# One group of batch 1's first product in Strassen's form, batch 2's second half dealt to later slots, one slot skipped in batch 7's features

## The chip, the cores and the metric

The kernel runs on one core of a Trainium2 chip. Times are device microseconds (us) of a whole execution. Three runs of the kernel before gave 289.28, 289.88 and 290.69 us, a median of 289.88. One further execution was profiled. It took 289.9 us, of which the profile's span, from the first to the last instruction, is 288.1 us. Of the core's engines PE multiplies matrices, DVE (vector) and ACT (scalar) do elementwise work, POOL does casts and additions on data that is not in PSUM, and SP issues most of the DMAs.

## The reference

For each of 8 batches (8 heads, 576 positions, 64 channels a head) an attention without softmax is computed, and its output goes through a mixer with a low-rank step and two large products:

```python
q_p, k_p = phi(q, cos_w, sin_w), phi(k, cos_w, sin_w)    # relu(x)*cos and relu(x)*sin, side by side
kv  = einsum('bhsf,bhsd->bhfd', k_p, v);  z = sum(k_p, axis=2)
x   = einsum('bhsf,bhfd->bhsd', q_p, kv) / (einsum('bhsf,bhf->bhs', q_p, z)[..., None] + 1e-06)
u   = x + (x.T @ U @ V).T                                # x as (576, 512); rank 32
out = u + relu(u @ w_ch1) @ w_ch2                        # w_ch1: 512x2048, w_ch2: 2048x512
```

The first product, `u @ w_ch1`, and the second, with `w_ch2`, are most of the arithmetic.

## The kernel before, in words

**Tiling.** A batch's 576 positions are four chunks of 128 (c = 0 to 3) and a tail of 64 (c = 4). The 2048 hidden columns are 16 blocks j of 128. Chunks 0 to 3 of a batch run through the first product as 512 columns. The tails of two batches are put together as 128 columns and run by themselves (`g1_tail`, `g2_tail`).

**Slots.** The order of PE's work is written out by hand as a list of slots. `first_units(b)` lays the 16 slots of a batch's first product, `second_units(b)` the 14 half-parts of its second product, and `lay_all` puts them one behind the other. Batch 1's first product is slots 32 to 47, the tail product of batches 0 and 1 is 48 to 51, batch 1's second product is 52 to 65, the second tail product is 66 to 69, and batch 2's first product begins at slot 70. Everything else (features, attention, u, transposes, loads, forms) is put beside a slot by number: `put(at, ...)`. Each engine runs its instructions strictly in the order in which the slots and what lies beside them emit them; semaphores make it wait for the others.

**A first-product slot in plain form** is `g1_main(b, j)`: four matmuls of 512 columns into one PSUM bank of the pool `g` (three banks, `G3`), and a ReLU on ACT into `hid`. **A group m in Strassen's form** (`g1_part(b, m, part)`, seven parts) does four blocks j with 28 matmuls of 256 columns instead of 16 of 512. It needs four differences of u, `uT_form(b, n)` (line 608, tile `tb`), and four of the weights, `w1_form` (line 591, tile `sa`), both on DVE. The results of the parts 1, 6 and 5 are copied by ACT to `pw` (line 114), part 3 gets its ReLU on ACT, and the parts 2, 7 and 4 are finished by an addition on DVE (line 678) and, for odd batches, a ReLU on DVE (line 675). `MIXED` says which groups of which batch are in Strassen's form; the eight slots of such a half hold four plain blocks (`s4` to `s7`) and the seven parts.

**Batch b+1 beside batch b.** While batch 1 is in its products, the attention of batch 2 is done beside it. Its features (`q_prep`, `k_prep`, lines 305 and 307: ACT or DVE, one chunk and one of cos and sin at a time) come first, then `kv_pair` at slot 43 (40 matmuls, line 364, copied out by DVE, line 116), then five `x_unit`s (8 matmuls, line 439, and three DVE instructions, lines 429, 430, 449), then `A_unit` (line 465, copied out by ACT), `u_va` (line 495), two `u_add`s on DVE (line 506) and two DMA transposes of u to `uT` (line 535, on SP's queue). The transposes of q of the next batch (lines 408 and 413) go on the same queue. The second product (`w_part`, line 892) needs the forms of `hid` that DVE makes (`hid_form`, line 857).

Of the kernel before, what the change touches and what calls it, by code (L numbers as in the profile page):

```python
# [17 lines left out]
def kernel(  # L18
# [100 lines left out]
    V_, A_, G_ = nc.vector, nc.scalar, nc.gpsimd  # L119
# [478 lines left out]
    def uT_form(b, n):  # L598
        if b not in tb:
            tb[b] = pool.tile([P, 4, 2, 256], BF16, tag="tb", bufs=1, name="tb")  # L600
        t = tb[b]
        a, b_ = (
            (uT_block(b, 0, 1), uT_block(b, 0, 0)),
            (uT_block(b, 1, 1), t[:, 0]),
            (uT_block(b, 1, 1), uT_block(b, 0, 1)),
            (uT_block(b, 1, 0), t[:, 1]),
        )[n]
        V_.tensor_tensor(out=t[:, n], in0=a, in1=b_, op=ALU.subtract)
# [203 lines left out]
                in_=o_s[i * TS : i * TS + TS, :],  # L812
            )

    MIXED = {2: (0, 2), 3: (0, 2), 4: (0, 2), 5: (0, 2), 6: (0, 2)}
    FULL = [b for b, ms in MIXED.items() if 2 in ms and b > 2]
    HD = DM // 2
    KB = NJ // 2
# [209 lines left out]
    def loads(b):  # L1028
        def thunk(dst, src):
            def go():  # L1030
                load_tail(dst, src, b)
                load_main(dst, src, b)

            return go

        return thunk(qst, q), thunk(kst, k), thunk(vst, v)
# [5 lines left out]
    def lay(units, in_second):  # L1042
        slots.extend(units)
        second.extend([in_second] * len(units))
# [5 lines left out]
    def first_units(b):  # L1050
        starts[b] = len(slots)

        def unit(names, m):
            def go():
                for n in names:
                    if n[0] == "s":
                        g1_main(b, 4 * m + int(n[1]))
                    else:
                        g1_part(b, m, int(n))

            return go

        for m in (0, 2):
            if m in MIXED.get(b, ()):
                lay([unit(n.split(), m) for n in (HALF if b > 2 else HALF2)], False)
            else:
                lay([lambda j=j: g1_main(b, j) for j in range(4 * m, 4 * m + 8)], False)
        for i in range(4 * (0 < b)):
            n = 12 + 2 * i if b == 1 else (9, 11, 17, 18)[i] if b in MIXED and b > 2 else 8 + i + (b == 2)
            beside.setdefault(starts[b] + n, []).append(  # L1070
# [60 lines left out]
    def attention_plan(b):  # L1131
        plan = []
        odd = b % 2 == 1

        def put(at, f, *a):
            plan.append((at, lambda: f(b, *a)))

        ops = [(f, c, i) for f in (q_prep, k_prep) for c in QORD for i in range(2)]
        if b == 2:
            for n, (f, c, i) in enumerate(ops):  # L1140
                if n < 8:
                    put((25, 26, 27, 28, 28, 29, 29, 30)[n], feature, f, c, i, A_)
                elif n < 10:
                    put(24 + n, feature, f, c, i, V_)
                else:
                    put(
                        (34, 34, 35, 36, 37, 38, 39, 39, 40, 41)[n - 10], feature, f, c, i,
                        A_ if n in (14, 17) else V_,
                    )
            V0 = 33  # L1150
            at_q, at_load = (32, 34, 36), (37, 42, 43)
            kv_at, x_at, a_at, u_at = 43, (44, 46, 48, 50, 52), 54, 55
            a_bank = O1
        else:
            F, G = starts[b - 2] + (20 if odd and b < B - 1 else 16), starts[b - 1]
            late = b in (4, 6)
            both = (0, 1, 2, 8) if late else (0, 1, 2) if b == 7 else (0, 1, 2, 10, 11, 12) if b > 3 else (1, 2, 10, 11, 12)
            for s_ in range(G - F + 2 * late):
                for eng in (A_, V_)[: 1 + (s_ in both)]:
                    if ops:  # L1160
                        put(F + s_, feature, *ops.pop(0), eng)
            V0 = starts[b - 2] + 9 if b > 3 else F + 1
            at_q, at_load = (F + 7, F + 8, F + 8) if late else (F + 5, F + 7, F + 7), (F + 8, F + (16 if late else 14), V0 + (8 if late else 5))
            if b == 7:
                at_q = (F + 5, F + 11, F + 11)
            if b == 6:
                at_q, at_load = (F + 7, F + 12, F + 12), (F + 12, F + 16, V0 + 8)
            if b == 3:
                at_q = (F + 6, F + 7, F + 8)
                at_load = (F + 11, F + 14, F + 14)  # L1170
            X0 = G - 2 if odd else G
            x_at = [
                X0 + i for i in ((2, 4, 6, 9, 11) if b == 3 else (2, 4, 6, 8, 10) if odd else (3, 5, 7, 9, 11))
            ]
            kv_at = X0
            if late:
                kv_at, x_at = G + 3, [G + i for i in (5, 8, 13, 16, 18)]
            elif b - 1 in FULL:
                kv_at, x_at = G + 1, [G + i for i in ODDX]
            elif b > 3 and b - 1 in MIXED:  # L1180
                kv_at, x_at = G + 1, [G + i for i in X5]
            a_at = x_at[4] + (3 if b in (4, 6) else 3 if b == 3 else 2)
            u_at = a_at + 1
            a_bank = X1S if b == 3 else OB
        for n, c in enumerate(QORD):
            put(V0 + n, v_prep, 0, H, (c,), (G_,))
        for at_, (c0, c1) in zip(at_q, ((4, 5), (0, 2), (2, 4))):
            put(at_, qtr_dma, c0, c1)
        put(kv_at, kv_pair, *X1)
        for n, c in enumerate(ORD):  # L1190
            put(x_at[n], x_unit, c, *((O1, X1)[n % 2] if b < 4 else X1))
        put(a_at, A_unit, *a_bank, A_)
        put(u_at, u_va, (0, *X1), (2, *O1) if b < 4 else (2, OA, OB))
        d0 = 2 if odd and b - 1 in FULL else 0
        put(u_at, u_add, d0)
        put(u_at + 2, u_add, 2 - d0)
        put(u_at + 2, utr_dma, d0, d0 + 2)
        put(u_at + 4, utr_dma, 2 - d0, 4 - d0)
        if odd:
            late_t = 3 if b == 5 and b - 1 in FULL else 0 if b - 1 in FULL else 1 if b - 1 in MIXED else 0  # L1200
            put(u_at + 3 + d0 + late_t, u_tail, *X1S)
            put(u_at + 4 + d0 + late_t, utr_dma, 4, 5)
        if b < B - 1:
            for at_, t in zip(at_load, loads(b + 1)):
                plan.append((at_, t))
        return plan
# [233 lines left out]
    def put(at, thunk):  # L1440
        todo.setdefault(at, []).append(thunk)
# [3 lines left out]
    for n in range(4):  # L1445
        for m in (0, 2):
# [4 lines left out]
            )  # L1451
        for b in MIXED:
            put(starts[b] + (-3, -2, 0, 2)[n], lambda b=b, n=n: uT_form(b, n))
# [7 lines left out]
    for b in range(2, B):  # L1461
        for at, t in attention_plan(b):
            put(at, t)
# [35 lines left out]
```

## Time and profile before

| what | value |
|---|---|
| median of three runs | 289.88 us |
| profiled execution, its time | 289.9 us |
| profiled execution, its span | 288.1 us |
| PE busy | 281.1 us, 98% of the span |
| DVE busy | 221.9 us, 77% |
| ACT busy | 180.9 us, 63% |
| POOL busy | 71.3 us, 25% |
| PE's granted clock | 9 tenths or more in all 40 slices |

Times in the trace are counted from the start of the span. A row of the timeline has the start, the length, the engine, the line, the operation, what it writes and reads, and how many such instructions were merged. What stands in brackets is how long the engine had been idle before, and what ended that. PE is pipelined and the ends of its matmuls are modelled, so two rows of PE can overlap; the distance between the starts is what a group of matmuls really takes. The same holds in a smaller measure on DVE, where the next instruction starts some 0.08 us before the end that the row shows.

### The profile page before, as it was taken

What the parts mean: (1) busy time and instruction counts of PE and PEld (TensorE: products, weight loads), DVE (VectorE), ACT (ScalarE), POOL (GpSimd) and SP (SyncE); (2) the same over time, 40 slices, a digit from 0 to 9 for tenths busy, and PEclk for the clock granted to TensorE, in tenths of its full rate; (3) what the DMA queues carried; (4) which work ended last, traced back from release to release, by engine and by line L of the source; (5) the groups of instructions that cost most, each with busy time, mean ns of one, the idle gap of its engine ahead of it and who ended that gap; (6) DMA issues with size and microseconds to landing.
All of it is one profiled execution on the core that took longest, in us unless ns stands there. A gap on an engine that the chain in (4) does not pass through costs nothing. (4 is left out here: it accounts for less than half of the span.)

```text
span 288.1 us, 7603 instructions
## 1 busy us (share of the span) xinstructions
PE 281.1 (98%) x3108; PEld 212.1 (74%) x3134; DVE 221.9 (77%) x452; ACT 180.9 (63%) x319; POOL 71.3 (25%) x111
## 2 busy tenths in 40 slices
PE   8999999999999999999999999999999999999995
PEld 6776455545887767876987767876978778899884
DVE  4979739997888899658885498858884689689864
ACT  2975651576687588876686588876797772177110
POOL 8330600050008305640015500351015000400140
PEclk9999999999999999999999999999999999999999
DMA  6999999999999999899929991499959200610023
GB/s 201 337 284 252 289 208 251 284 178 154 281 213 190 239 362 184 212 269 250 257 54 198 321 304 43 89 152 183 299 69 233 99 0 11 156 75 2 2 86 132
DMA packets 85447, 53.32 MB, mean 185 GB/s; under 512 B 53990, under 2 KB 83078, under 8 KB 85414
## 3 DMA queue, kind: packets, MB, share of 16 engines
q1 hardware_dynamic: 78998, 41.62, 62.5%
q0 software_dynamic: 6272, 11.17, 16.3%
q8 instruction: 24, 0.39, 0.6%
q10 hardware_dynamic: 144, 0.07, 0.1%
q14 instruction: 9, 0.07, 0.1%
HBM read 36.86 MB, written 9.44 MB: 161 GB/s over the span
## 5 line engine op out<-in xcount | busy, mean ns | idle before, releaser
L710 PE MATMUL g_ps<-uT,w_bf 128*128 128x512 bf16 x264 | 67.5, 379 | 0.7
L717 ACT ACTIVATE hid<-g_ps 128x512 bf16<-128x512 f32 x72 | 42.6, 597 | 24.3 <-PE g_ps L710 21.5
L912 POOL TENSOR_TENSOR o_sb<-o_sb,u_bf 128x512 f32<-128x512 f32 x21 | 25.8, 1242 | 111.0 <-DVE o_sb L912 111.0
L892 PEld LDWEIGHTS <-hid 128*128 128x128 bf16 x448 | 43.0, 98 | 5.7 <-DVE hid L857 0.2
L678 DVE TENSOR_TENSOR hid<-pw,be_ps 128x512 bf16<-128x512 f32 x42 | 28.8, 686 | 17.8 <-PE be_ps L653 10.1
L710 PEld LDWEIGHTS <-w_bf 128*128 128x128 bf16 x282 | 26.2, 98 | 22.0
L892 PEld LDWEIGHTS <-S 128*128 128x128 bf16 x336 | 32.2, 98 | 4.4
L114 ACT ACTIVATE pw<-al_ps 128x512 f32<-128x512 f32 x42 | 24.9, 595 | 15.6 <-PE al_ps L653 9.8
L892 PE MATMUL w_ps<-T,hid 128*128 128x256 bf16 x224 | 27.9, 273 | 0.0
L892 PE MATMUL w_ps<-w_bf,hid 128*128 128x256 bf16 x224 | 27.8, 273 | 0.0
L892 PE MATMUL w_ps<-T,S 128*128 128x256 bf16 x224 | 27.1, 273 | 0.0
L114 ACT ACTIVATE o_sb<-w_ps 128x512 f32<-128x512 f32 x21 | 12.5, 597 | 20.4 <-PE w_ps L892 14.1
L912 DVE TENSOR_TENSOR o_sb<-o_sb,w_ps 128x512 f32<-128x512 f32 x21 | 14.4, 685 | 14.2 <-PE w_ps L892 7.5
L653 PEld LDWEIGHTS <-sa 128*128 128x128 bf16 x224 | 20.7, 98 | 5.3 <-issue 0.3
L506 DVE TENSOR_TENSOR u_bf<-x_bf,va_ps 128x1024 bf16<-128x1024 bf16 (+1 forms) x20 | 19.5, 1000 | 2.3 <-PE va_ps L495 2.3
L449 DVE TENSOR_TENSOR x_bf<-x_ps,rec 128x512 bf16<-128x512 f32 x28 | 19.4, 691 | 1.0
L653 PEld LDWEIGHTS <-w_bf 128*128 128x128 bf16 x168 | 16.3, 98 | 4.1 <-issue 0.2
L116 POOL CAST v_ext<-vst 128x512 bf16<-128x512 f32 x24 | 16.5, 727 | 7.3 <-issue 3.3
L305 ACT ACTIVATE k_p<-kst,sinw 128x512 bf16<-128x512 f32 x26 | 18.0, 712 | 0.4 <-DMA kst<-in_k_dram 0.4
L653 PE MATMUL al_ps<-tb,sa 128*128 128x256 bf16 x112 | 16.8, 273 | 0.3
L741 PE MATMUL gt_ps<-uT_tl,w_bf 128*128 128x128 bf16 x256 | 16.4, 219 | 0.0
L781 PE MATMUL o_ps<-w_bf,hid 128*128 128x512 bf16 x61 | 15.3, 379 | 0.2
(192 smaller groups left out, 513.5 us busy)
## 6 DMA issues: line engine op xcount, KB each, us to landing
qst<-in_q_dram SPq DMA_DIRECT2D x14, 512.0 KB, 6.1
kst<-in_k_dram SPq DMA_DIRECT2D x14, 512.0 KB, 8.1
vst<-in_v_dram SPq DMA_DIRECT2D x12, 512.0 KB, 9.7
out_dram<-o_sb POOLq DMA_DIRECT2D x12, 512.0 KB, 6.5
w_bf<-in_moe_w_ch_dram POOLq DMA_DIRECT2D x8, 512.0 KB, 11.0
out_dram<-o_sb SPq DMA_DIRECT2D x4, 512.0 KB, 3.0
qst<-in_q_dram SPq DMA_DIRECT2D x2, 640.0 KB, 5.7
kst<-in_k_dram SPq DMA_DIRECT2D x2, 640.0 KB, 13.8
```

What stands on the lines that cost most here:

```text
L114: nc.scalar.activation(out=o, in_=i, func=AF.Copy, bias=0.0, scale=1.0)
L116: eng.tensor_copy(out=o, in_=i)
L305: nc.scalar.activation(out=o, in_=i, func=AF.Relu, bias=0.0, scale=w)
L449: nc.vector.tensor_tensor(out=x_of(b, c, rows).rearrange("p (g i d) -> p g i d", g=2, d=D), in0=view[:, :, :, 0:D], in1=rec[rows].unsqueez ...
L506: nc.vector.tensor_tensor(out=u_bf[b][:, d0 : d0 + n], in0=x_bf[b].rearrange("p c (d n) -> p d c n", n=P)[:, d0 : d0 + n], in1=t.rearrange ...
L653: nc.tensor.matmul(out=res[:, k_, :], lhsT=lhs[:, d, k_, :], rhs=rhs[:, d, :], start=(opens and k_ == 0 and d == 0), stop=(k_ == 1 and d = ...
L678: V_.tensor_tensor(out=o, in0=x, in1=res, op=ALU.add)
L710: nc.tensor.matmul(out=g_ps.rearrange("p (c t) -> p c t", c=4), lhsT=w1_bf[:, d, j * P : j * P + P], rhs=uT[b][:, d, :, :], start=(d == 0) ...
L717: nc.scalar.activation(out=hid[b][:, j, :], in_=g_ps, func=AF.Relu, bias=0.0, scale=1.0)
L741: nc.tensor.matmul(out=g_ps[:, jj, :], lhsT=w1_bf[:, d, j * P : j * P + P], rhs=uT_tl[pr][:, d, :], start=(d == 0), stop=(d == 3),)
L892: nc.tensor.matmul(out=res[:, g, :], lhsT=lhs[:, k_, g * P : g * P + P], rhs=rhs[:, k_, :], start=(opens and k_ == 0 and g == 0), stop=(k_ ...
L912: eng.tensor_tensor(out=o_, in0=x, in1=y, op=ALU.add)
```

## The change

There are three parts.

1. `MIXED` gets the entry `1: (2,)`: the second group of eight blocks of batch 1 (slots 40 to 47) has its blocks 8 to 11 in Strassen's form. By the loop over `MIXED`, four `uT_form`s are put at the slots 29, 30, 32 and 34; the weight forms for this group were already there, for batch 2.
2. In batch 2's plan two feature steps of k are dealt to ACT at other places (steps 12 and 14 in place of 14 and 17), the fourth and fifth `x_unit` go from the slots 50 and 52 to 51 and 53, `A_unit` from 54 to 57 and `u_va` from 55 to 58. What hangs on `u_at` (the two `u_add`s and the two transposes) moves with it, to the slots 58 and 60 and 60 and 62. On SP's queue the first transpose of `u` now comes behind the next batch's transposes of q's tail and of the first half of q, and the second behind that of q's second half.
3. In batch 7's features the slot `F + 3` takes no feature, so that the features that followed come one slot later.

```diff
-    MIXED = {2: (0, 2), 3: (0, 2), 4: (0, 2), 5: (0, 2), 6: (0, 2)}
+    MIXED = {1: (2,), 2: (0, 2), 3: (0, 2), 4: (0, 2), 5: (0, 2), 6: (0, 2)}
...
                     put(
                         (34, 34, 35, 36, 37, 38, 39, 39, 40, 41)[n - 10], feature, f, c, i,
-                        A_ if n in (14, 17) else V_,
+                        A_ if n in (12, 14) else V_,
                     )
...
-            kv_at, x_at, a_at, u_at = 43, (44, 46, 48, 50, 52), 54, 55
+            kv_at, x_at, a_at, u_at = 43, (44, 46, 48, 51, 53), 57, 58
...
             for s_ in range(G - F + 2 * late):
+                if b == 7 and s_ == 3:
+                    continue
                 for eng in (A_, V_)[: 1 + (s_ in both)]:
```

## The prediction

> **What bounds the kernel now.** I read the busy shares first, then PE's waits, then the stretches around batch 1's first product.
>
> ```profile
> PE 281.1 (98%) x3108; PEld 212.1 (74%) x3134; DVE 221.9 (77%) x452; ACT 180.9 (63%) x319; POOL 71.3 (25%) x111
> ```
>
> ```profile
> PE w_ps L202 <- DVE zero L125: 1.2, 1, 1.2
> PE va_ps L495 <- ACT A_sb L114: 0.4, 1, 0.4
> PE xz L1219 <- ACT k_p L305: 0.4, 1, 0.4
> ```
>
> ```profile
> core 0: us, PE busy (x) PEld busy (x) DVE busy (x) ACT busy (x) POOL busy (x), PEclk, DMA share, GB/s
> 64.54:67.99 3.45, 3.45 (x17) 1.57 (x16) 2.95 (x7) 3.06 (x6) 0.00 (x0) 1.00 1.27 112
> 67.99:73.27 5.28, 5.23 (x72) 3.29 (x72) 3.43 (x9) 2.39 (x4) 0.00 (x0) 1.00 1.01 183
> 73.27:83.80 10.53, 10.53 (x173) 9.40 (x172) 9.26 (x19) 7.30 (x13) 0.00 (x0) 1.00 1.12 291
> ```
>
> PE is busy for 98% of the span, and the list of its waits has three entries, 2.0 us in all. So PE's own work sets the end: less of it is a gain one for one, and what any other engine does costs nothing until PE waits for it. Two of the waits are at the start; the middle one is a `u_va` that waits for ACT's copy of A, and part 3 of the change touches it. The stretches (batch 1's slots 40 to 43, 44 to 47, then the tail product and the first slots of the second product) show how near the others are to becoming the bound: DVE is busy for 2.95 of 3.45 us, 3.43 of 5.28 and 9.26 of 10.53. PE's clock is full throughout.
>
> **Part 1a, PE's work.** The chain that ended last has both kinds of matmul group without a wait between them:
>
> ```profile
> 223.93 0.44 PE al_ps L653 x4
> 226.54 0.86 PE g_ps L710 x4
> ```
>
> Four plain blocks are 4 x 0.86 = 3.44 us; the seven parts that replace them are 7 x 0.44 = 3.08. PE loses 0.4 us of work. All of it is gained ahead of `kv_pair`: the slots 40 to 43 held four blocks (3.44), and now hold the parts 1, 6, 2 and two blocks (3 x 0.44 + 2 x 0.86 = 3.04); the slots 44 to 47 go from 3.44 to 4 x 0.44 + 2 x 0.86 = 3.48.
>
> **Part 1b, DVE's new work ahead of `kv_pair`.** Four `uT_form`s come in at the slots 29 to 34. In the timeline (DVE, with the rows of the other engines that meet it):
>
> ```profile
> 55.88 0.60 ACT L114 ACTIVATE uT<-u 128x512 bf16<-128x512 f32 x1 [1.71 <-DVE uT L116]
> 56.36 0.42 DVE L591 TENSOR_TENSOR sa<-w_bf,sa 128x512 bf16<-128x512 bf16 x1
> 59.00 1.22 DVE L506 TENSOR_TENSOR u_bf<-x_bf,va_ps 128x1024 bf16<-128x1024 bf16 x1 [0.63 <-PE va_ps L495]
> 59.50 2.96 POOL L116 CAST v_ext<-vst 128x512 bf16<-128x512 f32 x4
> 60.14 1.10 DVE L833 TENSOR_TENSOR T<-w_bf 128x1024 bf16<-128x1024 bf16 x1
> 64.83 0.67 DVE L833 TENSOR_TENSOR T<-w_bf,T 128x1024 bf16<-128x1024 bf16 x1
> 67.02 0.47 DVE L307 TENSOR_SCALAR k_p<-kst,sinw 128x512 bf16<-128x512 f32 x1
> 69.42 0.70 DVE L116 CAST kv<-kv_ps 128x520 bf16<-128x520 f32 x1 [1.93 <-PE kv_ps L364]
> ```
>
> ```profile
> 63.68 4.48 PE L710 MATMUL g_ps<-uT,w_bf 128*128 128x512 bf16 x20
> 67.99 0.28 PE L364 MATMUL kv_ps<-v_ext,k_p 128*128 128x65 bf16 x4
> 69.20 1.03 PE L710 MATMUL g_ps<-uT,w_bf 128*128 128x512 bf16 x3
> ```
>
> What one form takes, and what an addition with its ReLU takes, is read from the starts in later batches, where they stand back to back, and the spread of the forms from their group:
>
> ```profile
> 94.36 0.41 DVE L591 TENSOR_TENSOR sa<-sa,w_bf 128x512 bf16<-128x512 bf16 x1
> 94.69 0.41 DVE L608 TENSOR_TENSOR tb<-uT,tb 128x512 bf16<-128x512 bf16 x1
> ...
> 134.31 0.68 DVE L678 TENSOR_TENSOR hid<-pw,be_ps 128x512 bf16<-128x512 f32 x1
> 135.03 0.29 DVE L675 TENSOR_SCALAR hid<-hid 128x512 bf16<-128x512 bf16 x1
> 135.24 0.69 DVE L857 TENSOR_TENSOR S<-S,hid 128x1024 bf16<-128x1024 bf16 x1
> ```
>
> ```profile
> L608 DVE TENSOR_TENSOR tb<-uT,tb x12: 411/420/1126, 94.7 to 253.5; 128x512 bf16<-128x512 bf16 x12
> ```
>
> A form takes 0.33 us from start to start, an addition with ReLU 0.93 (134.31 to 135.24). The first form also waits for ACT's copy of uT, which ends at 56.48, while DVE was free at 56.36: about 0.17 with the handover. So 4 x 0.33 + 0.17 = 1.5 us of new DVE time lies between 56.36 and the last `k_p` feature. The only slack there is the 0.63 us of idle time at 59.00; from there to 67.49 (67.02 + 0.47) DVE runs without a gap. The last feature, which `kv_pair` needs, ends 0.87 later, at 68.36. PE, which has gained 0.4, is at `kv_pair` at 64.54 + 3.04 = 67.58 (63.68 + 0.86 is the start of slot 40). It waits some 0.8 us and starts `kv_pair` at about 68.4 where it was 67.99: 0.4 later than before, the gain spent and as much again.
>
> Bounds: below, no wait at all, if DVE keeps pace (the slots 40 to 47 then end 0.4 earlier); above, forms as slow as some are beside POOL. `T` took 1.10 us while POOL cast v and 0.67 after; the slowest form took 1.126. One form, that of slot 34, falls where POOL's casts, themselves later behind a later store, will be; 0.3 to 0.4 more than 0.33 makes the start 68.8. I take 68.5, since three of the four lie ahead of the casts: +0.5 us. The Trainium skill (SBUF — State Buffer, Who interferes with whom) says that a DVE instruction with two SBUF inputs shares a read interface with a GpSimd instruction that reads SBUF, and that the one issued second is blocked until the first ends. Both inputs of a form are in SBUF, so by that rule the form of slot 34 waits for up to a whole cast, 0.74 (2.96 / 4), an estimate that would put the start at up to 69.1 and the sum at up to 290.6. The two rows of `T` agree with the rule's direction: 0.43 more beside the casts.
>
> The additions cost PE nothing here. The first (part 2) fits into the gap of 1.93 us ahead of the copy of kv. That copy ends 0.9 after PE has issued `kv_pair` (69.42 + 0.70 against 69.20), and PE has the parts 5 and 7 (0.88) in between. ACT's count in these slots stays the same, four copies or ReLUs for four ReLUs. Of the k features beside these slots ACT keeps two and DVE six; ACT's come two slots earlier, where the ReLUs of three banks of `g` cover them (if they didn't, PE would wait for one feature, 0.7), and DVE's end no earlier than reckoned above.
>
> **Part 2, the later half.** DVE gets two more additions with ReLU, 1.86 us, and is 0.5 late. It had 5.28 - 3.43 + 10.53 - 9.26 = 3.1 us of idle time up to 83.80. So it fits, but tightly. The nearest customers:
>
> ```profile
> 78.43 0.69 DVE L857 TENSOR_TENSOR S<-S,hid 128x1024 bf16<-128x1024 bf16 x1
> 82.05 1.05 PE L892 MATMUL w_ps<-T,S 128*128 128x256 bf16 x8
> ```
>
> S was ready at 79.12, 2.9 us before PE took it. DVE reaches it at most 0.5 + 1.86 later, at 81.5, and less by whatever of its idle time lies before. PE comes to it at 82.05 + 0.5 less A and `u_va`, which no longer stand before it (about 0.5 each, an estimate from the `u_va` row below, 0.40, and the change of operands): 81.5. So DVE is just in time, or early by the idle time, about 0.6 us. The `x_unit` ahead of A ends as much later; three slots (3 x 0.87) of delay for A cover that. I count part 2 as nothing on PE. What it does to SP's queue:
>
> ```profile
> 83.40 1.38 SPq L535 DMA_TRANSPOSE uT<-u_bf  x1
> 86.22 1.44 SPq L535 DMA_TRANSPOSE uT<-u_bf  x1
> 87.77 5.20 SPq L408 DMA_TRANSPOSE q_pT<-q_p  x2
> 93.03 1.00 SPq L93 DMA_DIRECT2D qst<-in_q_dram  x1
> 96.15 1.02 PE L710 MATMUL g_ps<-uT,w_bf 128*128 128x512 bf16 x4
> ```
>
> ```profile
> DMA to landing us min/median/max: 3.0/3.4/4.9
> DMA to landing us min/median/max: 4.3/5.1/11.8
> ```
>
> The first landing row is that of `uT`, the second that of `q_pT`. The first transpose of u moves from 83.40 by 2.6 + 0.5 to about 86.5 and holds SP to 87.9; the transpose of q's second half now follows (2.6, half of 5.20) to 90.5; the second transpose of u starts then, in place of 86.22, and lands at 93.5 to 95.4. The form that reads it would start at 94.69 + 0.5 = 95.2, PE's plain block at 96.15 + 0.5 = 96.6. With the median, 93.9, nobody waits; with the longest, DVE waits 0.2 and PE still nothing. The transposes of q are read only after slot 70, and the loads behind them on SP start about 1 us earlier than at 93.03; neither costs.
>
> **Part 3.**
>
> ```profile
> 209.89 0.71 ACT L305 ACTIVATE q_p<-qst,sinw 128x512 bf16<-128x512 f32 x1
> 210.98 0.27 ACT L114 ACTIVATE A_sb<-a_ps 128x128 bf16<-128x128 f32 x1
> 211.30 0.40 PE L495 MATMUL va_ps<-A_sb,V_bf 32*128 32x128 bf16 x16 [0.39 <-ACT A_sb L114]
> ```
>
> The feature at 209.89 now comes after A's copy. Taking 0.6 us away from ahead of that copy removes the 0.39 us that PE sat idle; what is late next is PE's own second product, so 0.39 is gained. ACT does the feature later, with more than a slot in hand before batch 7's kv. Bounds: 0 and 0.39.
>
> **Sum.** +0.5 (the net of -0.4 work and 0.9 wait) - 0.39 = +0.1 us against the profiled execution's 289.9, which stands with the median, 289.88. Forecast 290.0 us.
>
> **The rivals.** *DVE keeps pace, no wait at `kv_pair`*: -0.4 - 0.39 = -0.8, 289.1 us. For it: 0.5 us between the last feature and `kv_pair` in the trace, and forms at 0.33; against: DVE has no other gap after 59.00.
>
> *The second transpose of u lands late, slower.* It now waits behind a transpose of q, and those took up to 11.8 us to land. From a landing at 96.6 on PE waits for it, and DVE, which stands in order before the form, holds the additions behind it. With a landing as long as 7 us (90.5 + 7 = 97.5) PE loses 0.9 at its plain block and about as much again until DVE has caught up: 290.0 + 1.8 = 291.8. Against: no transpose of u took more than 4.9, and the next loads of q, k and v (from 93.03 before) stand behind it on SP.
>
> *Weight loads show.* There are 28 loads for 16, at 98 ns each (the 64.54 stretch has 1.57 us in 16); unhidden, twelve more cost 1.2 and the gain of 0.4 is no gain: 291.6. Against: 0.44 / 4 = 110 ns a matmul is no more than half of 0.86 / 4 = 215. The Trainium skill (TensorE: Matmul & The Clock Gate, Back-to-back issue gap) gives 131 ns for a sustained matmul of 512 columns and 81 for 128, by which 28 short ones would cost at least as much as 16 long ones (estimate 2.3 to 2.1 us); the trace's 215 and 110 do not agree.
>
> *Part 3 does nothing*, another copy holding ACT: 290.4.
>
> **How the numbers follow.** Forecast 0.55, DVE keeps pace 0.22, late transpose (or DVE's backlog reaching PE at S) 0.14, weight loads 0.02, part 3 without effect 0.07. The range goes from 288.8 (the gain of both, less the 0.3 that medians vary) to 291.6, and leaves out about 0.1 on either side together with the runs' scatter. 0.5%, 1.45 us, is about what can be told from no change. Faster than 288.4 needs more than the two gains together: 0.05. Slower than 291.3 is the late transpose, the weight loads, and a share of the forecast with several margins gone: 0.17. The rest, 0.78, is the same.
>
> **What the profile after would show.** A wait of PE at `kv_pair` (line 364) for a k feature on DVE, 0.7 to 1.2 us; 28 more matmuls of line 653 at 0.44 for four; no wait at line 495; no idle time of DVE between 59 and the copy of kv. Wrong would make it: no wait at line 364; a wait of line 710 or of DVE's forms for `uT` near 95; a wait of line 892 for S.

## The result, and the profile after

| | before | after |
|---|---|---|
| median of 22 runs each | 290.03 us | 290.60 us |
| lowest to highest | 289.28 to 291.88 us | 290.12 to 292.11 us |
| profiled execution: time, span | 289.9, 288.1 us | 290.39, 288.2 us |

The ratio of after to before is 1.0026, with a 95% interval of 1.0014 to 1.0038: the changed kernel is slower by 0.75 us (0.4 to 1.1; the two medians are 0.57 apart), less than the 0.5% that counts as a difference here. The forecast was 290.0. Three executions in the experiments below, two of part 3 alone (its profiled one among them) and one of the first two forms behind the additions, fell into a slower state of the chip (spans of 292.0 to 292.6 us) and are left out of all medians, ratios and readings.

The page of the changed kernel, its busy shares, and the list of PE's waits (engine, line, what it waited for, then us in total, times, longest):

```profile
span 288.2 us, 7669 instructions
...
PE 283.0 (98%) x3146; PEld 214.2 (74%) x3146; DVE 223.8 (78%) x462; ACT 180.8 (63%) x319; POOL 72.4 (25%) x111
```

```profile
PE w_ps L202 <- DVE zero L125: 1.2, 1, 1.2
PE kv_ps L364 <- DVE k_p L307: 0.3, 1, 0.3
PE g_ps L710 <- DVE o_sb L789: 0.2, 1, 0.2
```

PE's wait for ACT at line 495 is gone, and so is the one at line 1219, which lies at the start and comes and goes from run to run. Two new waits for DVE are there: the forecast one at `kv_pair`, and one at line 710, which no step of the prediction had. PE's busy time (281.1 before, 283.0 after) is no measure of its work here: the page before counts 3108 matmuls for 3134 weight loads, the page after 3146 for 3146, so some matmuls are missing from the first.

The single profiled executions differ in their starts and in late loads, so the spans alone tell little. A cleaner ruler is the stretch from the start of slot 32 (batch 1's first product) to the start of slot 70 (batch 2's). Before, from PE's timeline:

```profile
56.74 1.89 PE L710 MATMUL g_ps<-uT,w_bf 128*128 128x512 bf16 x8
...
95.45 0.60 PE L653 MATMUL al_ps<-uT,w_bf 128*128 128x256 bf16 x4
```

After:

```profile
56.86 1.03 PE L710 MATMUL g_ps<-uT,w_bf 128*128 128x512 bf16 x4
58.04 1.02 PE L710 MATMUL g_ps<-uT,w_bf 128*128 128x512 bf16 x4 [0.15 <-DVE o_sb L789]
...
64.97 0.60 PE L653 MATMUL al_ps<-uT,w_bf 128*128 128x256 bf16 x4
65.41 1.03 PE L710 MATMUL g_ps<-uT,w_bf 128*128 128x512 bf16 x4
...
68.04 0.26 PE L364 MATMUL kv_ps<-v_ext,k_p 128*128 128x65 bf16 x3
68.64 0.20 PE L364 MATMUL kv_ps<-v_ext,k_p 128*128 128x65 bf16 x1 [0.34 <-DVE k_p L307]
...
69.76 0.60 PE L653 MATMUL al_ps<-tb,sa 128*128 128x256 bf16 x4
...
96.02 0.60 PE L653 MATMUL al_ps<-uT,w_bf 128*128 128x256 bf16 x4
```

Before it takes 95.45 - 56.74 = 38.71 us, after 96.02 - 56.86 = 39.16: 0.45 us more. Where they come from is read from the distances between starts. Slot 32 to slot 33 takes 1.18 us, where one plain block takes 0.86: PE lost 0.3. Slots 40 to 43 take 68.04 - 64.97 = 3.07 us in place of 67.99 - 64.54 = 3.45: the gain of 0.4, and a part takes 0.44 (64.97 to 65.41) as forecast. `kv_pair` takes 69.76 - 68.04 = 1.72 in place of 69.20 - 67.99 = 1.21: another 0.5 lost. From there to slot 70 both take the same (26.26 and 26.25). So +0.3 - 0.4 + 0.5 = +0.4.

What DVE and POOL did meanwhile:

```profile
56.63 0.42 DVE L608 TENSOR_TENSOR tb<-uT 128x512 bf16<-128x512 bf16 x1
56.97 0.42 DVE L591 TENSOR_TENSOR sa<-w_bf,sa 128x512 bf16<-128x512 bf16 x1
57.31 0.68 DVE L789 TENSOR_TENSOR o_sb<-u_bf,o_ps 128x512 f32<-128x512 bf16 x1
57.90 0.42 DVE L608 TENSOR_TENSOR tb<-uT,tb 128x512 bf16<-128x512 bf16 x1
...
60.45 2.96 POOL L116 CAST v_ext<-vst 128x512 bf16<-128x512 f32 x4
62.90 0.79 DVE L608 TENSOR_TENSOR tb<-uT,tb 128x512 bf16<-128x512 bf16 x1
63.61 0.47 DVE L307 TENSOR_SCALAR k_tl<-kst,cosw 64x512 bf16<-64x512 f32 x1
...
68.11 0.47 DVE L307 TENSOR_SCALAR k_p<-kst,sinw 128x512 bf16<-128x512 f32 x1
```

The first form stands ahead of DVE's addition of line 789, which reads a bank of `g` that still holds batch 0's second product. That addition ends at 57.99, and PE's second block starts at 58.04. The last feature of k ends at 68.11 + 0.47 = 68.58, and PE goes on at 68.64.

### The profile page after: what moved, and what is told of

It is laid out like the page before. It is cut to its first block, busy times and chain, and to the rows that moved or that the text cites. A ratio compares the mean times of both kernels' runs of the same rounds, so it can differ in the third digit from the quotient of the medians.

```text
span 288.2 us, 7669 instructions
## 1 busy us (share of the span) xinstructions
PE 283.0 (98%) x3146; PEld 214.2 (74%) x3146; DVE 223.8 (78%) x462; ACT 180.8 (63%) x319; POOL 72.4 (25%) x111
## 4 chain that ended last, share of the span: by engine, by line
PE 93%; DVE 4%; issue 1%; ACT 0%; DVEq 0%
PE w_ps L892 30%; PE g_ps L710 17%; PE al_ps L653 9%; PE be_ps L653 7%; PE gt_ps L741 5%; PE o_ps L781 4%; PE w_ps L202 3%; PE x_ps L439 3%; PE kv_ps L364 3%; PE ot_ps L801 2%; PE ot_ps L994 2%; PE a_ps L465 1%; PE va_ps L495 1%; DVE u_bf L506 1%; PE t_ps L382 1%; PE t_ps L394 1%
## 5 line engine op out<-in xcount | busy, mean ns | idle before, releaser
L710 PE MATMUL g_ps<-uT,w_bf 128*128 128x512 bf16 x266 | 66.8, 379 | 0.2 <-DVE o_sb L789 0.2
L717 ACT ACTIVATE hid<-g_ps 128x512 bf16<-128x512 f32 x68 | 40.2, 597 | 23.2 <-PE g_ps L710 22.9
L678 DVE TENSOR_TENSOR hid<-pw,be_ps 128x512 bf16<-128x512 f32 x45 | 30.9, 686 | 17.7 <-PE be_ps L653 10.0
L114 ACT ACTIVATE pw<-al_ps 128x512 f32<-128x512 f32 x45 | 26.7, 595 | 16.7 <-PE al_ps L653 11.4
L653 PEld LDWEIGHTS <-sa 128*128 128x128 bf16 x240 | 22.2, 98 | 5.9 <-issue 0.5
L116 POOL CAST v_ext<-vst 128x512 bf16<-128x512 f32 x24 | 17.5, 767 | 7.4 <-DMA vst<-in_v_dram 4.2
L653 PE MATMUL al_ps<-tb,sa 128*128 128x256 bf16 x120 | 18.0, 272 | 0.0
L305 ACT ACTIVATE k_p<-kst,sinw 128x512 bf16<-128x512 f32 x25 | 17.2, 712 | 0.0
L755 POOL DMA_DIRECT2D out_dram<-o_sb x12 | 7.6, 631 | 32.2 <-DVE o_sb L789 24.0
```

What stands on the lines that cost most here:

```text
L114: nc.scalar.activation(out=o, in_=i, func=AF.Copy, bias=0.0, scale=1.0)
L116: eng.tensor_copy(out=o, in_=i)
L305: nc.scalar.activation(out=o, in_=i, func=AF.Relu, bias=0.0, scale=w)
L653: nc.tensor.matmul(out=res[:, k_, :], lhsT=lhs[:, d, k_, :], rhs=rhs[:, d, :], start=(opens and k_ == 0 and d == 0), stop=(k_ == 1 and d = ...
L678: V_.tensor_tensor(out=o, in0=x, in1=res, op=ALU.add)
L710: nc.tensor.matmul(out=g_ps.rearrange("p (c t) -> p c t", c=4), lhsT=w1_bf[:, d, j * P : j * P + P], rhs=uT[b][:, d, :, :], start=(d == 0) ...
```

## The experiments

The ruler of the section above is used throughout: "the stretch" is the time from the start of slot 32 to that of slot 70 in the run's profiled execution. Kernels that do the same there agree in it within 0.02 us, which the medians can't do.

**Part 1 alone.**

```diff
-    MIXED = {2: (0, 2), ...}
+    MIXED = {1: (2,), 2: (0, 2), ...}
```

> Part 1 alone (Strassen's form, the old slots of A and u). Theory: PE work -0.4, a wait of 0.2 to 0.3 for a bank of g behind an addition of line 789 near 58 us, a wait of 0.6 at kv_pair, and then a wait of 1 to 2 us at A near 81 us because DVE's x chain is late: 1.5 to 2.5 us slower than before, ratio 1.005 to 1.009. Rival: DVE catches up by then, and A does not wait: 0.5 us slower, ratio 1.002.

Measured: 291.73 us, ratio 1.0078 (1.0055 to 1.0102). PE's rows:

```profile
65.68 1.03 PE L710 MATMUL g_ps<-uT,w_bf 128*128 128x512 bf16 x4
67.19 0.60 PE L653 MATMUL al_ps<-tb,sa 128*128 128x256 bf16 x4 [0.48 <-ACT pw L114]
...
82.29 0.24 PE L465 MATMUL a_ps<-x_tl,U_bf 128*32 128x128 bf16 x4 [0.94 <-DVE x_bf L449]
```

Without part 2 PE waits for DVE at A, as expected, and for a bank that ACT's copy to `pw` frees late; this wait stands in the place of the expected one at `kv_pair`, which isn't there. The stretch is 97.40 - 57.13 = 40.27 us. With parts 1 and 2 together (below) both waits are gone, so part 2 is what makes room for the additions.

**Part 2 alone**: only the lines of batch 2's plan.

```diff
-                        A_ if n in (14, 17) else V_,
+                        A_ if n in (12, 14) else V_,
...
-            kv_at, x_at, a_at, u_at = 43, (44, 46, 48, 50, 52), 54, 55
+            kv_at, x_at, a_at, u_at = 43, (44, 46, 48, 51, 53), 57, 58
```

> Part 2 alone (batch 2's later A, u and transposes; nothing in Strassen's form in batch 1). Theory: no effect on PE, span 288.1, ratio 1.000 within 0.0005; the second transpose of u lands near 95.5 and the form that reads it waits on DVE up to 1 us, PE does not. Rival: the late landing costs PE in some executions: ratio 1.001 to 1.003 though the profile may show none of it.

Measured: 290.02 us, ratio 1.0000 (0.9985 to 1.0016). All of PE's waits are these, and the stretch is 95.61 - 56.89 = 38.72:

```profile
PE w_ps L202 <- DVE zero L125: 1.2, 1, 1.2
PE xz L1219 <- ACT k_p L305: 0.4, 1, 0.4
```

Part 2 costs nothing by itself, as forecast; DVE waits 0.6 us for u's second transpose, PE doesn't. But PE's wait at line 495 isn't there either, and this kernel hasn't got part 3. So a kernel without part 3 need not have that wait.

**Part 3 alone.**

```diff
             for s_ in range(G - F + 2 * late):
+                if b == 7 and s_ == 3:
+                    continue
```

> Part 3 alone (the skipped slot in batch 7's features). Theory: the wait of PE at line 495 near 211 us, 0.39 us, is gone and nothing takes its place: 0.4 us faster than before in the profile (span 287.7) and in the median, ratio 0.9986. Rival: another copy holds ACT, or a later wait gives it back: ratio 1.000, span 288.1.

Measured: 289.85 us, ratio 0.9997 (0.9979 to 1.0015). The 0.39 us that I had booked for part 3 would be 0.9987. The interval holds that as well as no change; the traces of kernels without part 3, in the next experiment, say more.

**Parts 1 and 2, without part 3.**

```diff
-                if b == 7 and s_ == 3:
-                    continue
```

> Parts 1 and 2 without part 3. Theory: what the changed kernel lost up to 211 us stays: 0.57 us in the profile (span 288.7), and 0.4 us over the changed kernel: median about 291.0, ratio to before 1.003 to 1.004. Rival: part 3 is worth nothing, and this equals the changed kernel, ratio 1.0026.

Measured: 290.77 us, ratio 1.0034 (1.0022 to 1.0045). The ratio falls where the theory put it, but its interval holds the rival's 1.0026 too, and the profile doesn't show the 0.39. Its two waits for DVE are those of the whole change, and its stretch is 95.90 - 56.73 = 39.17. In batch 6, too, it is nearly undisturbed. From PE's timeline, the distance from the matmuls of line 892 to those of line 495 is 1.07 us; it is 0.98 with nothing to wait for (in part 2 alone, for one) and 1.43 in the profile before:

```profile
210.30 1.05 PE L892 MATMUL w_ps<-w_bf,hid 128*128 128x256 bf16 x8
211.37 0.40 PE L495 MATMUL va_ps<-A_sb,V_bf 32*128 32x128 bf16 x16
```

Why the profile before had a wait there is in ACT's timeline of before, some 4 us earlier:

```profile
207.08 0.72 ACT L305 ACTIVATE q_p<-qst,cosw 128x512 bf16<-128x512 f32 x1 [0.48 <-DMA qst<-in_q_dram]
```

A load of q was late there, and ACT idle for 0.48 us; ACT carried the delay through four features and what stands between them to the copy of A. In part 2 alone ACT does the same features without that gap and copies A at 210.66, against 210.98. A third size of the delay is in a run that is described below (the kernel before with more matmuls at the start; ACT, then PE):

```profile
207.93 0.72 ACT L305 ACTIVATE q_p<-qst,cosw 128x512 bf16<-128x512 f32 x1 [0.16 <-DMA qst<-in_q_dram]
```

```profile
211.04 1.05 PE L892 MATMUL w_ps<-w_bf,hid 128*128 128x256 bf16 x8
212.16 0.41 PE L495 MATMUL va_ps<-A_sb,V_bf 32*128 32x128 bf16 x16
```

Here PE's distance is 1.12. By the starts of ACT's rows, its feature comes 0.45 us late in the profile before, 0.13 in this run, 0.09 with parts 1 and 2, and not at all in the other three traces without part 3 (part 1 alone, part 2 alone, more fills on DVE); PE loses 0.45, 0.14, 0.09 and nothing. So the wait is the lateness of this load, and part 3 can gain no more than that. Outside the stretch the spans come out alike: 288.2 - 39.17 = 249.0 us here, 288.2 - 39.16 = 249.0 with part 3.

**The first two forms behind the additions.** The theory: the wait for a bank of `g` and the wait at `kv_pair` are one delay of DVE, seen twice.

```diff
-            put(starts[b] + (-3, -2, 0, 2)[n], lambda b=b, n=n: uT_form(b, n))
+            put(starts[b] + ((-1, -1, 0, 2) if b == 1 else (-3, -2, 0, 2))[n], ...)
```

> The changed kernel with batch 1's first two differences of u put at slot 31, behind the additions of line 789. Theory: both new waits have one cause, DVE's lateness. The wait of line 710 for a bank of g (0.2 to 0.3 us) goes, but DVE ends the last k feature at the same time, so PE only waits longer at kv_pair (0.3 + 0.3): no change, span 288.2 to 288.6, ratio to before 1.002 to 1.003. Rival: the waits are separate prices: 0.3 us faster than the changed kernel, ratio 1.0015.

Measured: 290.67 us, ratio 1.0030 (1.0000 to 1.0059).

```profile
57.78 1.89 PE L710 MATMUL g_ps<-uT,w_bf 128*128 128x512 bf16 x8
...
68.65 0.48 PE L364 MATMUL kv_ps<-v_ext,k_p 128*128 128x65 bf16 x3
69.72 0.20 PE L364 MATMUL kv_ps<-v_ext,k_p 128*128 128x65 bf16 x1 [0.59 <-DVE k_p L307]
...
70.85 0.60 PE L653 MATMUL al_ps<-tb,sa 128*128 128x256 bf16 x4
```

The slots 32 and 33 are one group of eight again, without a wait between them, and `kv_pair` takes 70.85 - 68.65 = 2.20 us, 1.0 more than before. The two losses of 0.3 and 0.5 have become one of 1.0, and the stretch is 97.11 - 57.78 = 39.33: the delay stays, as the theory had it, and is paid in one place. (The whole span is longer here also because PE waited 0.6 us for a late load of weights before slot 32.)

**Two later products for T.** Instead of the forms, DVE's work for T (line 833) leaves the slots ahead of `kv_pair`.

```diff
-        todo.setdefault((19, 21, 23, 25, 27, 28, 33, 36)[i], []).append(
+        todo.setdefault((19, 21, 23, 25, 27, 28, 59, 61)[i], []).append(
```

> The changed kernel with the last two forms of w_ch2 (line 833) moved from the slots 33 and 36 to 59 and 61, which takes 1.5 us of DVE out of the stretch ahead of kv_pair. Theory: kv_pair no longer waits for line 307; the gain of 0.4 in PE work is left, less the 0.3 at the bank of g: 0.7 us faster than the changed kernel, 0 to 0.1 faster than before, ratio 0.9995 to 1.000. Rival: something else than DVE's lateness makes the difference: ratio stays at 1.0026.

**Both moves together**, the last two diffs in one kernel.

> The changed kernel with both moves, the differences of u at slot 31 and the forms of line 833 at 59 and 61. Theory: neither wait is left, and PE's 0.4 us of saved work shows: ratio to before 0.9986, span 287.7 or, where before's span has the 0.39 us at line 495, the same 287.7. Rival: the freed time goes into a new wait (S at line 892, or the copy of kv): ratio 1.000.

Measured: T later, 290.45 us, ratio 1.0006 (0.9981 to 1.0032); both, 290.41 us, ratio 1.0007 (0.9983 to 1.0032). PE's timeline with both moves:

```profile
67.83 0.29 PE L364 MATMUL kv_ps<-v_ext,k_p 128*128 128x65 bf16 x4
...
84.51 1.92 PE L892 MATMUL w_ps<-T,S 128*128 128x256 bf16 x16
87.05 1.03 PE L892 MATMUL w_ps<-T,hid 128*128 128x256 bf16 x8 [0.62 <-DVE T L833]
```

and DVE's:

```profile
85.75 1.24 DVE L833 TENSOR_TENSOR T<-w_bf 128x1024 bf16<-128x1024 bf16 x1
```

The waits for a bank of `g` and for k are gone, which shows that DVE's queue ahead of `kv_pair` was their cause. In their place PE waits for T: from 84.51 to 87.05 are 2.54 us for 16 matmuls, where 1.75 is the rule in the kernel after (85.24 to 86.99). That is 0.8 lost, and the stretch is 96.07 - 56.96 = 39.11. With T alone moved it is 96.35 - 57.23 = 39.12: 0.3 lost at the bank of `g`, and 0.5 at T. So in three orders of DVE's work PE loses the same 0.8 in other places. That it is the same each time is partly chance: in the kernel with both moves T's product takes 1.24 us, where it takes 0.73 with T alone moved. Neither theory's gain (0.7 us, and a ratio of 0.9986) came; the second one's rival, a new wait, did, at T instead of S. The medians are 0.15 to 0.2 lower than with the change as it was, which is less than the intervals can tell.

**u's transposes ahead of q's.** They come late after the change (below); here SP issues both before those of both halves of the next batch's q (q's tail stays first).

```diff
-                at_q = (F + 6, F + 7, F + 8)
+                at_q = (F + 6, F + 10, F + 10)
```

> The changed kernel with the two transposes of batch 2's u ahead of both halves of the next q on SP's queue. Theory: the wait of DVE for uT near 96 us (2.3 us) goes, PE gains nothing, as it never waited there: ratio 1.002 to 1.003. Rival: the late landing costs PE in some executions: median 0.2 us or more below the changed kernel, and fewer executions above 291.

Measured: 291.48 us, ratio 1.0049 (1.0020 to 1.0078). Neither what I expected nor the rival came: the interval still holds the expected 1.002 to 1.003, but the median is 0.9 us above that of the changed kernel, and 10 of 12 executions are above 291 us where 7 of 22 were. The transposes of q start later (a row has the shortest, median and longest time on SP's queue in ns, then the first and the last start in us; after, then this run):

```profile
L408 SPq DMA_TRANSPOSE q_pT<-q_p x4: 1619/3194/5294, 85.2 to 126.1; - x4
```

```profile
L408 SPq DMA_TRANSPOSE q_pT<-q_p x4: 1531/3937/4912, 89.5 to 127.4; - x4
```

But the profiled execution was the fastest of the twelve (span 288.3; the median is 289.35), its stretch is 39.18 us, and PE waits for no transpose in it. What the other executions lost isn't in any profile, so the cause stays open.

**The time outside the span.** An execution takes longer than its span, and by amounts that fall into groups. The spans are on record to 0.1 us, which alone spreads a difference by 0.05 either way:

| kernel | weight loads on PE, instructions on DVE | time less span: median (range) | median span |
|---|---|---|---|
| before (96 runs) | 3134, 452 | 1.79 (1.73 to 1.86) | 288.2 |
| part 2 alone | 3134, 452 | 1.77 (1.75 to 1.83) | 288.25 |
| part 3 alone | 3134, 452 | 1.77 (1.72 to 1.85) | 288.0 |
| part 1 alone | 3146, 462 | 1.97 (1.80 to 2.12) | 289.85 |
| parts 1 and 2 | 3146, 462 | 2.15 (2.10 to 2.17) | 288.6 |
| after | 3146, 462 | 2.15 (2.09 to 2.20) | 288.45 |
| more matmuls at the start, before | 3146, 452 | 1.77 (1.74 to 1.85) | 288.3 |
| fewer matmuls at the start, after | 3133, 462 | 2.14 (2.09 to 2.20) | 288.35 |
| more fills on DVE, before | 3134, 463 | 1.85 (1.82 to 1.89) | 288.35 |

The other variants of the changed kernel have medians of 2.13 to 2.17. So 0.36 us of what the change costs lie outside the span. The last three rows are the runs that tried two explanations, the count of PE's instructions and that of DVE's (`keep_warm` multiplies zeros at the start, before the first features):

```diff
-    keep_warm(4, "X", 1)
-    keep_warm(72, "X", 1, P)
+    keep_warm(2, "X", 1)        # more: in the kernel before
+    keep_warm(86, "X", 1, P)
...
-    keep_warm(4, "X", 1)
-    keep_warm(72, "X", 1, P)
+    keep_warm(7, "X", 1)        # fewer: in the kernel after
+    keep_warm(56, "X", 1, P)
...
+    for _ in range(11):         # fills: in the kernel before
+        V_.memset(ones[:, 0:2], 1.0)
```

> The kernel before, with 12 more matmuls on zeros ahead of the first features (2 of 512 columns fewer, 14 of 128 more, so that their sum of columns is nearly the same), 6,294 records on PE and its weight loads instead of 6,270, as in the changed kernel. Theory: the 0.35 us by which the changed kernel's executions exceed their spans more than before (2.14 against 1.79 us) goes with the number of PE's instructions. Then this kernel's executions exceed their spans by 2.1 us and it takes about 290.35 us (1.001 of before), the span within 0.2 us of before's. Rival: it goes with something else of the change; then the excess stays at 1.8 us and the ratio is 1.000.

> The changed kernel, with 13 fewer matmuls on zeros ahead of the first features (3 of 512 columns more, 16 of 128 fewer), 6,268 records on PE and its weight loads. If the time outside the span goes with the number of PE's instructions, it falls from 2.14 to 1.79 us and the ratio to before from 1.0026 to about 1.0014 (290.25 us). If it goes with DVE's instructions or another part of the change, it stays at 2.14 us and the ratio at 1.0026. The kv step's wait and the wait for a bank of g are as in the changed kernel in either case (0.3 and 0.2 us).

> The kernel before, with 11 small fills (128 x 2) on DVE at the start, so that DVE has 451 instructions instead of 440, as in the changed kernel; PE's are unchanged. If the time outside the span goes with DVE's instructions, it rises from 1.79 to 2.14 us (290.35 us, 1.001 of before). If it goes with PE's, it stays at 1.79 us and the ratio is 1.000; the fills themselves take under 0.1 us each, while DVE waits for the first loads, and should not show in the span by more than 0.2 us.

Measured: 290.10 us, ratio 1.0002 (0.9984 to 1.0021); 290.48 us, 1.0015 (1.0001 to 1.0028); 290.21 us, 1.0006 (0.9988 to 1.0025). The theory of PE's count falls both ways: more instructions without the change leave it at 1.77, fewer with the change at 2.14. So does DVE's: eleven more give 0.06, not 0.36. Nor is it the total: the run with 1.77 has 13 weight loads and as many matmuls more than the run with 2.14, and only 10 instructions of DVE fewer. It comes with part 1, since neither part 2 nor part 3 alone has it (of the six runs of part 1 alone three lie at 1.80 to 1.89 and three at 2.05 to 2.12); by what, stays open. The stretches of the three are 38.71, 39.17 and 38.71 us, so in the stretch nothing moved.

**All three mends.**

```diff
-        todo.setdefault((19, 21, 23, 25, 27, 28, 33, 36)[i], []).append(
+        todo.setdefault((19, 21, 23, 25, 27, 28, 56, 63)[i], []).append(
...
+            put(starts[b] + ((-1, -1, 0, 2) if b == 1 else (-3, -2, 0, 2))[n], ...)
...
-    keep_warm(4, "X", 1)
-    keep_warm(72, "X", 1, P)
+    keep_warm(7, "X", 1)
+    keep_warm(56, "X", 1, P)
```

> The changed kernel with all three mends: the two forms for slots 32 and 33 placed behind DVE's addition (slot 31), the two last products for T of group 2 placed at slots 56 and 63, and 13 fewer matmuls on zeros at the start. If the waits for a bank of g and for the last feature of k were the whole loss in the span, and PE's count that outside of it, the span is 287.8 us and the time 289.6 us (0.9985 of before, with the bounds 0.997 and 1.000), and PE has no wait for DVE's T or k. Rival: DVE is late for T instead (0.3 to 0.6 us at the third group's second product, as in the run that moved T's products to 59 and 61) and the time stays at 290.0 to 290.4 us (1.000 to 1.001).

Measured: 290.63 us, ratio 1.0018 (1.0000 to 1.0036). The rival won, and by more than its price. PE and DVE:

```profile
88.62 1.04 PE L892 MATMUL w_ps<-T,hid 128*128 128x256 bf16 x8
90.98 1.03 PE L892 MATMUL w_ps<-T,hid 128*128 128x256 bf16 x8 [1.32 <-DVE T L833]
```

```profile
88.82 0.69 DVE L912 TENSOR_TENSOR o_sb<-u_bf,w_ps 128x512 f32<-128x512 bf16 x1 [0.57 <-PE w_ps L892]
89.43 1.50 DVE L833 TENSOR_TENSOR T<-w_bf,T 128x1024 bf16<-128x1024 bf16 x1
```

The later of T's products, now at slot 63, stands on DVE behind an addition that itself waits for PE, and PE waits for it in turn: 2.36 us between the starts in place of 0.87, 1.5 lost. Of these, 0.8 are the product's own length: it took 1.50 us here, and 0.68 (at 88.78) in the kernel with both moves; why, isn't shown. No arrangement that I tried beats the kernel before.

## Why the prediction was right, and where it was not

The time came out inside the range, on the side "the same", 0.6 us above the forecast. The mechanism of the largest term, DVE late ahead of `kv_pair`, is borne out; one term failed and one was missing, and both errors point the same way.

- **PE's work, -0.4**: right. The slots 40 to 43 went from 3.45 to 3.07 us. The weight loads show nowhere; four matmuls of 256 columns take 0.44 with their loads.
- **DVE late by the forms, 0.9 of waiting**: right in cause and nearly in sum, wrong in place. The last feature ends at 68.58 (forecast 68.36) and DVE has no idle time from 59 on. The step that was missed is the first place where DVE's lateness is felt: I looked for who needs the k features, and passed over the additions of line 789 that stand behind the first form and still hold a bank of `g`. PE paid 0.3 there and 0.5 at `kv_pair`, 0.8 in all against 0.9. The wait that the page shows at `kv_pair` (0.3) is therefore below the forecast 0.7 to 1.2.
- **The form of slot 34 beside POOL**: it took 0.79 in place of 0.42 and 0.71 from start to start, 0.4 more than its neighbours, the upper end of the bound. By the rule of the Trainium skill (SBUF — State Buffer, Who interferes with whom) it would have been blocked until POOL's last cast ended at 63.41, and delayed by 0.5 (an estimate from the two rows). The trace agrees with the direction and shows a little less. That the casts are what slows it is shown by two of the experiments: where the same form starts behind the last cast (at 64.36 with the first two forms behind the additions, the casts ending at 63.56; at 62.52 with both moves, the casts ending at 62.48), it takes 0.41.
- **Part 2, nothing on PE**: right, and tight as said:

```profile
80.53 0.69 DVE L857 TENSOR_TENSOR S<-S,hid 128x1024 bf16<-128x1024 bf16 x1
80.81 1.91 PE L892 MATMUL w_ps<-T,S 128*128 128x256 bf16 x16
```

  S ends at 81.22, some 0.5 us before PE's second group of eight needs it (80.81 + 0.87).
- **u's second transpose**: the rival came close. It was issued at 91.28 (forecast 90.5):

```profile
91.28 2.02 SPq L535 DMA_TRANSPOSE uT<-u_bf  x1
...
96.02 0.43 DVE L608 TENSOR_TENSOR tb<-uT,tb 128x512 bf16<-128x512 bf16 x1 [2.34 <-DMA uT<-u_bf]
```

  It landed 4.7 us later, near the longest of the row shown in the prediction. DVE came to the form at 93.7, 1.5 us sooner than forecast, and stood 2.3 us for the transpose. A wait of DVE's forms for `uT` was one of the signs that would make the prediction wrong; it came, but PE paid nothing for it. With 0.7 us more the landing would have reached PE's block at 96.72.
- **Part 3, -0.39**: wrong, and this is the step that failed. The row was real, but its size was that of one execution, in which ACT had stood 0.48 us for a late load. In five other traces without part 3 PE loses 0.14 us once, 0.09 once, and nothing three times. The sign "no wait at line 495" came true by luck: in the profile after that load came in time, and without a late load there is no wait there without part 3 either.
- **Outside the span, +0.36**: no term of the sum had it.

Put together: +0.45 in the stretch and +0.36 outside it are +0.8, within the measured 0.4 to 1.1. The medians of the spans are only 0.25 apart (0.5 at the lower quarter of the executions, 0.4 at the upper); the middle half of the executions of the kernel before is spread over 0.9 us. The forecast of +0.1 was the same +0.5 in the stretch, less a gain that wasn't there. What the runs leave open is why part 1 adds time outside the span, and why u's transposes ahead of q's make the kernel slower.

## What to carry to other kernels

Before a wait in a profile is booked as a gain, follow it back one more step: if it starts at a late DMA, another execution may not have it. When work is put on an engine that is in order, list everybody who waits for what stands behind it, and first of all who waits for a buffer that it still has to empty. And where a change moves tenths of a microsecond, measure a stretch between two starts on the engine that sets the end: it repeated within 0.02 us where whole executions scatter by more than 1.

## What the runs showed of the hardware

The idle time in a row's brackets is less than what is lost. At slot 33 it says 0.15 where the starts lie 0.3 further apart than usual, at `kv_pair` 0.34 for 0.5, for T 0.62 for 0.8. In these three about 0.17 are missing: the row of a group of four shows 1.03 us where the next start follows after 0.86, and the idle time counts from the end that the row shows. At line 495 before it was 0.39 for 0.45, so the difference isn't a constant. With POOL's casts beside it a form of 128 x 512 took 0.79 us, behind them 0.41. And the time of an execution beyond its span isn't one constant: 1.8 us for some of these kernels and 2.15 for others, each run within 0.08 of the median of its kernel, part 1 alone excepted.
